# Top-32 attention with a routed expert layer on one core: VectorE's choices and weighting moved behind the rank, sums of marks made to wait for them

## The chip, the cores and the metric

One NeuronCore of a Trainium2 chip runs the whole kernel. The metric is the device time of one execution in microseconds. The kernel before was timed three times, 1264.31 to 1267.04 us, with a median of 1265.7 us.

## The reference

```python
scores = scale * np.matmul(q, k.transpose(0, 1, 3, 2))          # 8 batches, 8 heads, 576 x 576, depth 64
kth = np.partition(scores, -top_k, axis=-1)[..., -top_k:-top_k + 1]   # top_k = 32
scores = np.where(scores >= kth, scores, -1000000000.0)
attn = softmax(scores); x = attn @ v                             # rows of 512 = 8 heads x 64
logits = x @ w_gate; e_idx = np.argmax(logits, axis=1)           # one of 8 experts a row
out[rows of e] = gate_w * sigmoid(x @ w_output_gate)[e] * (relu(x @ w1[e]) @ w2[e])
```

Each of the 4608 rows keeps, for each head, its 32 largest scores of 576; the attention output is sent to the one expert that its gate prefers (512 to 1024 to 512, float32), weighted by the gate's probability and a sigmoid.

## The kernel before, in words

**Steps.** The rows form 36 tiles of 128 queries, the heads four pairs. A step `i` (the loop of line 919) is one tile and one pair of heads, 144 steps in all and four more for what trails behind. Every engine gets its instructions in the order in which the program writes them, so a step is an order written out by hand, in which pieces of neighbouring pairs are interleaved.

**A pair's way.** TensorE forms the scores of pair `i + 1` at the top of step `i` (`scores`, L293), ScalarE copies them out of PSUM (L301). VectorE takes the eight largest of each of eight groups of 72 columns (`gmax`, MAX8, L320), a step ahead. `rank(i)` draws from these the 24 largest scores in three rounds (MAX8 L328, MATCH_REPLACE8 L331). `below(i)`: ScalarE marks what lies below the 24th with a Sign and counts it (L355), GpSimd adds marks and scores to a sum (`w`, L358), and `window` takes eight more of the sum with a MAX8 over 576 columns (L370). `choose` picks the 32nd largest of the row by the count (two tiny SCALAR_TENSOR_TENSORs, L381); `weigh` multiplies the exponentials (`exps`, ScalarE, L365) by "score is at least the 32nd" and sums them (L397).

In the first 36 steps (`LONE`) the second head of a pair is weighted in another way: `choose` also writes the negated 32nd value (`less`, L385), `veil` has ScalarE make a Sign of score less that value (L404) and GpSimd add it to the score (L407), and `unveil` takes ScalarE's Exp of that with its sum (L413), one step later.

Two steps after its rank a pair is transposed by TensorE in three parts (`flip`, L423: four blocks, one, four), each copied out by ScalarE (L431); two PSUM buffers serve the three parts, so the third part waits for the copy of the first. `attend` (L455, every second step) multiplies by the values, and ScalarE copies the result (L457).

**The order inside a step before.** Scores of `i + 1`; rank of `i` with three fills (a fill runs one queued small operation of the routing); scaling of rows; `below(i)`; `unveil(i - 2)`; attend, flips, a piece of an expert (`heavy`), Exps of `i`; then on VectorE `window(i - 1)` twice, `gmax(i + 1)`, a fill, `choose(i - 1)`, a fill, `weigh(i - 1)`; then gathers and scatters; `veil(i - 1)`; three fills.

**Experts.** When a group of tiles has been attended, `route` queues the small operations of its routing. For each slot (128 rows of one expert) the two weight matrices are loaded by SP (`fetch_w1` L704, `fetch_w2` L709) as soon as the slot stands in `order`; the list of its rows (`fetch_id`, L721) and the rows themselves (`fetch_x`, a GpSimd gather, L729) follow, TensorE transposes them (`turn`, L739), and a slot is worked off in four pieces, one a step (`up` L750 twice, `down` L765 twice). `later` queues slow GpSimd work with an estimated cost and a due time, and `run_slow` runs it from a budget at each step. For the first two groups the slots are fixed; for the other six a slot table (`slot_table`, some 32 tiny GpSimd operations) says which expert a slot serves, and SP reads it for the loads. Before, `route` queues the scatters of row ids first and the table behind them, and `queue_slots` extends `order` when both are done. The last nine slots and some before them are worked off behind the 144 steps.

Of the kernel before, what the change touches and what calls it, by code (L numbers as in the profile page):

```python
# [16 lines left out]
ALU = mybir.AluOpType  # L17
# [6 lines left out]
P = 128  # L24
# [8 lines left out]
DMAS = 2.2  # L33
MORE = 3.2
# [5 lines left out]
def tile_topk_attention_moe(  # L40
# [11 lines left out]
    nc = tc.nc  # L52
# [25 lines left out]
    ids = dram.tile([NID, 4], I32, name="ids")  # L78
# [12 lines left out]
    ENDS, EARLY, LEAST = zip(*sorts) if sorts else ((), (), ())  # L91
# [103 lines left out]
    def run(exact, stack):  # L195
# [25 lines left out]
        def later(what, cost, f, due):  # L221
            queued[0] += 1
            slow.append((step[0] + due, queued[0], what, cost, f))
            slow.sort()

        def run_slow(budget, kinds):

            for x in [x for x in slow if x[2] in kinds]:
                if spent[0] + x[3] > budget:
                    return  # L230
                slow.remove(x)
                spent[0] += x[3]
                x[4]()
# [7 lines left out]
        def waiting(what):  # L241
            return any(x[2] == what for x in slow)

        def fill(n=1):
            for _ in range(n):
                if urgent:
                    urgent.popleft()()
                elif small and small[0]() is not False:
                    small.popleft()
# [96 lines left out]
        def below(i):  # L346
            vs = VV[i][0]
            ep = wk.tile([P, 2, S], F32, name="ep", bufs=3)
            EP[i] = ep
            if not exact:  # L350
                n = wk.tile([P, 2], F32, name="n", bufs=3)
                SW[i] = ([], n)
                for a in range(2):
                    s, m = SC[i, a], marks[a]
                    nc.scalar.activation(m.bitcast(I8).rearrange("p (s b) -> p s b", b=2)[:, :, 1], s, AF.Sign,  # L355
                                         bias=vs[:, a, PIVOT - 1:PIVOT], scale=-(1.0 + 2.0 ** -20), accum_out=n[:, a:a + 1])
                    w = wk.tile([P, S], F32, name="w", bufs=3)
                    nc.gpsimd.tensor_tensor(w, s, m, op=ALU.add)  # L358
                    SW[i][0].append(w)

        def exps(i):
# [5 lines left out]
        def window(i, a):  # L367
            if exact:
                return
            nc.vector.max(out=VV[i][0][:, a, 24:32], in_=SW[i][0][a])  # L370

        def kth_col(i, a):
            return VV[i][0][:, a, TOPK - 1:TOPK] if exact else KTH[:, 2 * i + a:2 * i + a + 1]

        def choose(i):
# [10 lines left out]

            nc.gpsimd.tensor_copy(NEAR[:, i], vs[:, :, PIVOT - 1:PIVOT + 2:2])

        def weigh(i):
            t, hp = divmod(i, NHP)  # L390
            if hp == 0:
                SM[t] = st.tile([P, H], F32, name="sums", bufs=3)
            for a in (0, 1):
                if lone(i, a):
                    return
                e = EP[i][:, a, :]
                nc.vector.scalar_tensor_tensor(e, SC.pop((i, a)), kth_col(i, a), e, op0=ALU.is_ge, op1=ALU.mult,  # L397
                                               accum_out=SM[t][:, 2 * hp + a:2 * hp + a + 1])
            del VV[i]

        def veil(i):
# [407 lines left out]
        def queue_slots(g, n, rows):  # L809
            flush("x")  # L810
            assert rows_done[0] >= rows
            if g not in FIXED:
                order.extend((g, k, rows) for k in range(n))
            listed[0] += n
            known[0] = step[0] + (0 if had["id"] == cur[0] and not heavy else 1)
# [3 lines left out]
        def ids_known():  # L819

            ahead("id", fetch_id, listed[0] - cur[0])
            assert had["id"] - cur[0] <= NLIST - 2
# [68 lines left out]
        scores(0)(((0, 1), (1, 2)))  # L891

        def route(g):
            small.extend(group_route(g, LGT[g]))
            if g < NGRP - 1:
                def some(part):
                    for f in part:
                        f()
                if g in FIXED:
                    order.extend((g, k, (GROUPS[g][-1] + 1) * P) for k in range(EARLY[g]))  # L900
                    parts = [settle(FIXED[g])]
                else:
                    ops = slot_table(g, False)
                    parts = [ops[x:x + 4] for x in range(0, len(ops), 4)]

                def tables():
                    for part in parts:
                        later("ids", 0.18 * len(part), lambda part=part: some(part), 1)
                small.append(tables)
                small.append(lambda: not waiting("ids"))  # L910
                small.append(lambda: queue_slots(g, EARLY[g], (GROUPS[g][-1] + 1) * P))
                small.append(lambda: step[0] >= known[0] and ids_known())

        LGT = {}
        gi = 0
# [3 lines left out]
        for i in range(NSTEP + 4):  # L919
            t, hp = divmod(i, NHP)  # L920
            step[0] = i
            if i + 1 < NSTEP:
                scores(i + 1)()
            for r in range(3):
                if i < NSTEP:
                    rank(i, r)
                    if r == 0:
                        shift(i)
                fill(1)
            spent[0] = 0.0  # L930
            run_slow(SUMS, ("x",))
            spent[0] = 0.0
            if i < NSTEP:
                below(i)
            if 2 <= i < NSTEP + 2:
                unveil(i - 2)
            early, late = [], []
            if 4 <= i < NSTEP + 4 and i % 2 == 0:
                early.append(attend(i - 4))
            if 2 <= i < NSTEP + 2:  # L940
                early.append(flip(i - 2, 0))
                early.append(flip(i - 2, 1, side_start()))
            if i >= NSTEP + 2:
                extra = side_start()
                if extra:
                    early.append(extra(ps_t.tile([P, 4, P], F32, name="pst")))

            room = not uses
            ahead_of_slot()
            heavy_start()  # L950
            ev = heavy_piece()
            if ev:
                late.append(ev)
            if 2 <= i < NSTEP + 2:
                late.append(flip(i - 2, 2))
            ev = turn_ahead() if room else None
            if ev:
                late.append(ev)
            for f in early:
                f()  # L960
            if i < NSTEP:
                exps(i)
            for f in late:
                f()
            if 1 <= i <= NSTEP:
                window(i - 1, 0)
                window(i - 1, 1)
            if i + 1 < NSTEP:
                gmax(i + 1, 0)
                gmax(i + 1, 1)  # L970
            fill(1)
            if 1 <= i <= NSTEP:
                choose(i - 1)
                fill(1)
                weigh(i - 1)
            ahead("x", fetch_x, 2, "id", 1)
            run_slow(DMAS if i < LONE else MORE, ("ids", "out"))
            if 1 <= i <= NSTEP:
                veil(i - 1)
            side_use()  # L980
            fill(3)
            if i < NSTEP:
                if hp == 0 and t + 2 < NTT:
                    load_q(t + 2)
                if i == 0:
                    small.extend(([] if exact else setup()) + [clear_ids])
                jj = t % 9
                b2 = t // 9 * 2
                for j0, b in ((0, b2 + 1), (5, b2 + 2)):
                    n = (jj - j0) * NHP + hp  # L990
                    if b < NB:
                        if n == 1:
                            load_k(b)
                        if n == 6:
                            load_v(b)
            if i >= 3 and (i - 3) % NHP == NHP - 1:
                tt = (i - 3) // NHP
                if tt == GROUPS[gi][0]:
                    LGT[gi] = st.tile([P, max(map(len, GROUPS)), 16], F32, name="lg", bufs=2)
                tile_rows(tt, gi, LGT[gi], tt - GROUPS[gi][0])  # L1000
                if tt == GROUPS[gi][-1]:
                    gi += 1
# [6 lines left out]
        def background():  # L1009
            step[0] += 1  # L1010
            extra = side_start()
            if extra:
                extra(ps_t.tile([P, 4, P], F32, name="pst"))()
                side_use()
            fill(60)
            run_slow(1e9, ("ids", "x", "out"))

        tail[0] = True
        HL = {}
# [149 lines left out]
```

## Time and profile before

| what | value |
|---|---|
| median of three executions | 1265.7 us |
| the profiled execution | 1265.68 us |
| its span, first to last instruction | 1263.8 us |
| mean granted TensorE clock | 0.956 |
| PE busy | 1158.3 us (92%) |
| DVE busy | 1121.2 us (89%) |
| ACT busy | 961.5 us (76%) |
| POOL busy | 704.9 us (56%) |

PE is TensorE's matmuls, PEld its weight loads, DVE is VectorE, ACT ScalarE, POOL GpSimd, SP the engine that issues most DMAs. A row of a timeline reads: start and length in us, engine, line of the kernel, operation, output<-inputs, shapes, count, and in brackets how long the engine had been idle before and what ended that. In the table by stage each engine's busy time stands with its number of instructions. An engine that waits inside an instruction's own span is counted as busy.

### The profile page before, as it was taken

What the parts mean: (1) busy time and instruction counts of PE and PEld (TensorE: products, weight loads), DVE (VectorE), ACT (ScalarE), POOL (GpSimd) and SP (SyncE); (2) the same over time, 40 slices, a digit from 0 to 9 for tenths busy, and PEclk for the clock granted to TensorE, in tenths of its full rate; (3) what the DMA queues carried; (4) which work ended last, traced back from release to release, by engine and by line L of the source; (5) the groups of instructions that cost most, each with busy time, mean ns of one, the idle gap of its engine ahead of it and who ended that gap; (6) DMA issues with size and microseconds to landing.
All of it is one profiled execution on the core that took longest, in us unless ns stands there. A gap on an engine that the chain in (4) does not pass through costs nothing.

```text
span 1263.8 us, 30889 instructions
## 1 busy us (share of the span) xinstructions
PE 1158.3 (92%) x9771; PEld 889.1 (70%) x9771; DVE 1121.2 (89%) x6097; ACT 961.5 (76%) x1896; POOL 704.9 (56%) x1120
## 2 busy tenths in 40 slices
PE   4776676779999999999999999999989999999996
PEld 3554454457777677777777777777767777799995
DVE  6999999999999999999999999999989996363442
ACT  5899998888888888888888888888868886354542
POOL 5666666774547765586654775554865583321110
PEclk7788778889999999999999999999989999999998
DMA  5400033535545665575656655764076446799980
GB/s 138 78 18 18 18 101 123 179 86 183 184 159 168 202 211 170 179 219 182 211 188 205 218 193 196 226 205 159 10 266 229 159 159 233 254 397 366 360 328 21
DMA packets 113734, 227.46 MB, mean 180 GB/s; under 512 B 19206, under 2 KB 37894, under 8 KB 112528
## 3 DMA queue, kind: packets, MB, share of 16 engines
q1 hardware_dynamic: 104176, 205.67, 48.6%
q0 software_dynamic: 7552, 18.96, 4.4%
q8 instruction: 81, 1.33, 0.4%
q10 hardware_dynamic: 1824, 0.67, 0.3%
q14 instruction: 101, 0.83, 0.2%
HBM read 206.68 MB, written 20.69 MB: 180 GB/s over the span
## 4 chain that ended last, share of the span: by engine, by line
PE 51%; DVE 31%; issue 11%; ACT 3%; DMA 2%; POOL 2%; POOLq 0%; SPq 0%; ACTq 0%
PE pm L750 13%; PE pm L765 11%; DVE cand L320 10%; PE ps L293 8%; PE pst L423 8%; PE po L455 8%; DVE v L370 5%; DVE ep L397 5%; DVE x L381 3%; DVE cand L331 3%; DVE v L328 3%; DMA w1t<-in_w_dram 1%; PE pst L476 1%; ACT marks L355 1%; ACT s L301 1%
## 5 line engine op out<-in xcount | busy, mean ns | idle before, releaser
L358 POOL TENSOR_TENSOR w<-s,marks 128x576 f32<-128x576 f32 x288 | 362.8, 1281 | 170.3 <-ACT marks L355 166.4
L320 DVE MAX8 cand<-s 128x8 f32<-128x72 f32 x2304 | 322.3, 218 | 18.4 <-ACT s L301 18.0
L750 PE MATMUL pm<-xs,w1t 128*128 128x128 f32 x2560 | 299.6, 276 | 4.5 <-DMA w1t<-in_w_dram 3.6
L750 PEld LDWEIGHTS pm<-xs,w1t 128*128 128x128 f32 x2560 | 294.3, 193 | 6.1 <-DMA w1t<-in_w_dram 3.8
L423 PE MATMUL pst<-ident,ep 128*128 128x128 f32 x1296 | 212.5, 289 | 83.1 <-ACT ep L413 70.4
L423 PEld LDWEIGHTS pst<-ident,ep 128*128 128x128 f32 x1296 | 149.5, 144 | 166.1 <-ACT ep L413 77.4
L355 ACT ACTIVATE marks<-s,v 128x576 int8<-128x576 f32 x288 | 220.4, 769 | 21.8 <-DVE v L328 16.6
L431 ACT ACTIVATE pT<-pst 128x512 f32<-128x512 f32 (+1 forms) x432 | 196.6, 484 | 23.3 <-PE pst L423 15.1
L301 ACT ACTIVATE s<-ps 128x1152 f32<-128x1152 f32 (+1 forms) x145 | 163.0, 1125 | 57.8 <-PE ps L293 57.5
L370 DVE MAX8 v<-w 128x8 f32<-128x576 f32 x288 | 202.1, 743 | 0.2 <-issue 0.2
L765 PE MATMUL pm<-w2t,ht 128*128 128x512 f32 x448 | 202.0, 594 | 0.0
L293 PE MATMUL ps<-kst,qst 64*128 64x288 f32 (+1 forms) x1280 | 193.4, 455 | 5.1 <-ACT s L301 5.1
L397 DVE SCALAR_TENSOR_TENSOR ep<-s,kth,ep 128x576 f32<-128x576 f32 x252 | 197.3, 814 | 0.3 <-issue 0.3
L455 PEld LDWEIGHTS po<-pT,v 128*64 128x64 f32 x3200 | 167.9, 144 | 32.6 <-issue 32.6
L365 ACT ACTIVATE ep<-s,v 128x576 f32<-128x576 f32 x252 | 184.1, 781 | 0.5 <-POOL v L344 0.5
L455 PE MATMUL po<-pT,v 128*64 128x128 f32 (+1 forms) x3200 | 184.4, 274 | 0.0
L776 POOL DMA_INDIRECT out_dram<-y,idt x40 | 49.0, 1224 | 176.8 <-ACT y L772 163.5
L293 PEld LDWEIGHTS ps<-kst,qst 64*128 64x128 f32 (+1 forms) x1280 | 103.2, 187 | 50.1 <-issue 25.7
L765 PEld LDWEIGHTS pm<-w2t,ht 128*128 128x128 f32 x448 | 80.9, 190 | 81.0 <-issue 81.0
L328 DVE MAX8 v<-cand 128x8 f32<-128x16 f32 (+2 forms) x864 | 129.2, 190 | 0.0
L381 DVE SCALAR_TENSOR_TENSOR x<-left,n,v 128x8 f32<-128x8 f32 x288 | 113.4, 429 | 0.0
L331 DVE MATCH_REPLACE8 cand<-v,cand 128x16 f32<-128x16 f32 (+1 forms) x576 | 95.1, 174 | 0.0
(167 smaller groups left out, 1200.1 us busy)
## 6 DMA issues: line engine op xcount, KB each, us to landing
w1t<-in_w_dram SPq DMA_DIRECT2D x40, 2048.0 KB, 9.2
w2t<-in_w_dram SPq DMA_DIRECT2D x40, 2048.0 KB, 11.0
x_rows<-xu SPq DMA_DIRECT2D x36, 256.0 KB, 2.2
qst<-in_qa_dram SPq DMA_DIRECT2D x70, 128.0 KB, 10.3
v<-in_va_dram SPq DMA_DIRECT2D x8, 1024.0 KB, 5.8
kst<-in_ka_dram SPq DMA_DIRECT2D x14, 576.0 KB, 5.7
v<-in_va_dram SPq DMA_DIRECT2D x16, 64.0 KB, 6.2
ids<-far SPq DMA_DIRECT2D x1, 678.0 KB
```

Of the source, the lines that this page charges most:

```text
L293: nc.tensor.matmul(ps[qs, a, n, :288], Q[t][rows, hp, qs], K[b][rows, hp, cols], start=True, stop=True)
L320: nc.vector.max(out=c[:, 8 * g:8 * g + 8], in_=SC[i, a][:, g * GW:(g + 1) * GW])
L355: nc.scalar.activation(m.bitcast(I8).rearrange("p (s b) -> p s b", b=2)[:, :, 1], s, AF.Sign, bias=vs[:, a, PIVOT - 1:PIVOT], scale=-(1.0 ...
L358: nc.gpsimd.tensor_tensor(w, s, m, op=ALU.add)
L365: nc.scalar.activation(EP[i][:, a, :], SC[i, a], AF.Exp, bias=VV[i][0][:, a, 32:33], scale=SCALE)
L370: nc.vector.max(out=VV[i][0][:, a, 24:32], in_=SW[i][0][a])
L397: nc.vector.scalar_tensor_tensor(e, SC.pop((i, a)), kth_col(i, a), e, op0=ALU.is_ge, op1=ALU.mult, accum_out=SM[t][:, 2 * hp + a:2 * hp + ...
L423: nc.tensor.transpose(ps[:, c - c0, :], pt[:, c * P:(c + 1) * P], ident)
L431: nc.scalar.activation(x, ps[:, :n, :], AF.Copy)
L455: nc.tensor.matmul(po[a * 64:(a + 1) * 64, k, qs], lhs, rhs, start=half and not k and not m, stop=(c == 3 and k == 1 and m == len(TT[t]) - 1))
L750: nc.tensor.matmul(ph[:, f - f0, :], w[:, c, f * P:(f + 1) * P], XS[s][:, c, :], start=(c == 0), stop=(c == NC - 1))
L765: nc.tensor.matmul(PY[s], HT[s][:, f, :], w[:, f, :], start=(f == 0), stop=(f == NF - 1))
```

## The change

In a step, `choose(i - 1)`, two fills and `weigh(i - 1)` now come right behind the rank of `i`, then `below(i)` and `veil(i - 1)`, and only then the scaling of rows and `unveil(i - 2)`. GpSimd's first sum of marks in a step gets a dependency on the weighting of the pair before. `window(i)` now ends step `i`, behind `gmax(i + 1)`. In `route`, for the groups that need a slot table, the table's operations (a kind of their own, `table`) are queued ahead of the scatters, and `order` is extended as soon as the table is done; for the two fixed groups the order of things stays.

```diff
@@ below
                     w = wk.tile([P, S], F32, name="w", bufs=3)
-                    nc.gpsimd.tensor_tensor(w, s, m, op=ALU.add)
+                    x = nc.gpsimd.tensor_tensor(w, s, m, op=ALU.add)
+                    if LAST[0]:
+                        tc.add_manual_dep(x.ins, LAST[0].ins.name,
+                                          mybir.DependencyInfo(mybir.DependencyClass.Sync, mybir.DependencyReason.DATA),
+                                          reason="the weighting goes first")
+                        LAST[0] = None
@@ weigh
-                nc.vector.scalar_tensor_tensor(e, SC.pop((i, a)), kth_col(i, a), e, op0=ALU.is_ge, op1=ALU.mult,
-                                               accum_out=SM[t][:, 2 * hp + a:2 * hp + a + 1])
+                LAST[0] = nc.vector.scalar_tensor_tensor(e, SC.pop((i, a)), kth_col(i, a), e, op0=ALU.is_ge, op1=ALU.mult,
+                                                         accum_out=SM[t][:, 2 * hp + a:2 * hp + a + 1])
@@ queue_slots
-            if g not in FIXED:
+            if g == NGRP - 1:
                 order.extend((g, k, rows) for k in range(n))
@@ route
-            small.extend(group_route(g, LGT[g]))
+            ops = group_route(g, LGT[g])
+            small.extend(ops[:-1])
...
                 def tables():
                     for part in parts:
-                        later("ids", 0.18 * len(part), lambda part=part: some(part), 1)
-                small.append(tables)
+                        later("table", 0.18 * len(part), lambda part=part: some(part), 1)
+
+                def chosen():
+                    order.extend((g, k, (GROUPS[g][-1] + 1) * P) for k in range(EARLY[g]))
+                if g in FIXED:
+                    chosen()
+                    small.extend([ops[-1], tables])
+                else:
+                    small.extend([tables, ops[-1], lambda: not waiting("table"), chosen])
                 small.append(lambda: not waiting("ids"))
+                small.append(lambda: not waiting("table"))
                 small.append(lambda: queue_slots(g, EARLY[g], (GROUPS[g][-1] + 1) * P))
@@ a step
                 fill(1)
+            if 1 <= i <= NSTEP:
+                choose(i - 1)
+                fill(2)
+                weigh(i - 1)
+            if i < NSTEP:
+                below(i)
+            if 1 <= i <= NSTEP:
+                veil(i - 1)
             spent[0] = 0.0
             run_slow(SUMS, ("x",))
             spent[0] = 0.0
-            if i < NSTEP:
-                below(i)
             if 2 <= i < NSTEP + 2:
                 unveil(i - 2)
...
-            if 1 <= i <= NSTEP:
-                window(i - 1, 0)
-                window(i - 1, 1)
             if i + 1 < NSTEP:
                 gmax(i + 1, 0)
                 gmax(i + 1, 1)
-            fill(1)
-            if 1 <= i <= NSTEP:
-                choose(i - 1)
-                fill(1)
-                weigh(i - 1)
+            if i < NSTEP:
+                window(i, 0)
+                window(i, 1)
             ahead("x", fetch_x, 2, "id", 1)
-            run_slow(DMAS if i < LONE else MORE, ("ids", "out"))
-            if 1 <= i <= NSTEP:
-                veil(i - 1)
+            run_slow(DMAS if i < LONE else MORE, ("table", "ids", "out"))
```

More of the change, by code (lines that the diff above doesn't have):

```diff
@@ L387, in choose @@
             nc.gpsimd.tensor_copy(NEAR[:, i], vs[:, :, PIVOT - 1:PIVOT + 2:2])
+        LAST = [None]
         def weigh(i):
@@ L899, in route @@
                 if g in FIXED:
-                    order.extend((g, k, (GROUPS[g][-1] + 1) * P) for k in range(EARLY[g]))
                     parts = [settle(FIXED[g])]
                 else:
-                    ops = slot_table(g, False)
-                    parts = [ops[x:x + 4] for x in range(0, len(ops), 4)]
+                    table = slot_table(g, False)
+                    parts = [table[x:x + 4] for x in range(0, len(table), 4)]
                 def tables():
                     for part in parts:
-                        later("ids", 0.18 * len(part), lambda part=part: some(part), 1)
-                small.append(tables)
+                        later("table", 0.18 * len(part), lambda part=part: some(part), 1)
[6 more added lines that the diff above has]
+                    small.extend([tables, ops[-1], lambda: not waiting("table"), chosen])
                 small.append(lambda: not waiting("ids"))
+                small.append(lambda: not waiting("table"))
                 small.append(lambda: queue_slots(g, EARLY[g], (GROUPS[g][-1] + 1) * P))
                 small.append(lambda: step[0] >= known[0] and ids_known())
+            else:
+                small.extend(ops[-1:])
         LGT = {}
@@ L1015, in background @@
             fill(60)
-            run_slow(1e9, ("ids", "x", "out"))
+            run_slow(1e9, ("table", "ids", "x", "out"))
         tail[0] = True
```

## The prediction

> **What bounds the kernel now.** I read the page first for the span and the slices, then a table by stage, then the list of waits, and then the timelines of two places.
>
> ```profile
> span 1263.8 us, 30889 instructions
> PE   4776676779999999999999999999989999999996
> DVE  6999999999999999999999999999989996363442
> PEclk7788778889999999999999999999989999999998
> ```
>
> The slices show three stages: up to slice 8 VectorE is full and TensorE is not, and its clock is below full; then both are full; in the last six slices VectorE is half idle. The table by stage has the figures.
>
> ```profile
> 57.00:260.00 203.00, 142.15 (x1277) 99.11 (x1275) 198.56 (x1178) 183.12 (x389) 134.51 (x174) 0.84 0.22 71
> 305.00:1053.00 748.00, 742.43 (x6540) 559.63 (x6539) 740.24 (x4253) 612.12 (x1249) 466.78 (x782) 1.00 0.57 190
> 1053.00:1264.00 211.00, 197.79 (x1414) 175.09 (x1412) 92.26 (x146) 87.90 (x106) 43.71 (x59) 0.98 0.77 282
> ```
>
> Columns: length, then busy time of PE, weight loads, DVE, ACT and POOL, then the granted clock. I call the first stretch the veiled stage: there the second head of a pair is weighted by ScalarE (veil, unveil) and no expert work runs yet. The second is the mixed stage, the third the tail.
>
> In the mixed stage PE idles 748 - 742.43 = 5.6 us in all. Is a busy PE there a PE at its pace? One product block in the mixed stage, beside one of the tail:
>
> ```profile
> 947.09 3.74 PE L750 MATMUL pm<-xs,w1t 128*128 128x128 f32 x32
> 1109.80 6.19 PE L750 MATMUL pm<-xs,w1t 128*128 128x128 f32 x54
> ```
>
> 3.74/32 is 117 ns a matmul, 6.19/54 is 115 ns in the tail, where DVE is busy 92.26 of 211 us and cannot hold PE back. So the mixed stage goes at PE's pace, and a faster DVE is worth there at most the 5.6 us. The veiled stage has no such bound: PE is busy 142.15 of 203 us. Whom does it wait for?
>
> ```profile
> PE pst L423 <- ACT ep L413: 70.4, 26, 4.9
> PE pm L750 <- DMA w1t<-in_w_dram: 3.6, 1, 3.6
> ```
>
> Nearly all of its idle time ends with unveil (L413), ScalarE's Exp of the veiled head. ACT itself is busy 183.12 of the 203 us, so the stage can't become shorter than by 20 us.
>
> **The change part by part. 1. The stall that it removes.** The choices (L381) are tiny, yet some take long:
>
> ```profile
> L381 DVE SCALAR_TENSOR_TENSOR x<-left,n,v x288: 186/218/1972, 18.7 to 1061.7; 128x8 f32<-128x8 f32 x144
> 57.00:260.00 203.00, 25.32 (x116) 0.84 0.22 71
> 305.00:1053.00 748.00, 74.09 (x404) 1.00 0.57 190
> 711.89 2.25 DVE L320 MAX8 cand<-s 128x8 f32<-128x72 f32 x16 [0.19 <-ACT s L301]
> 712.68 2.52 POOL L358 TENSOR_TENSOR w<-s,marks 128x576 f32<-128x576 f32 x2 [1.37 <-ACT marks L355]
> 714.06 1.17 DVE L381 SCALAR_TENSOR_TENSOR x<-left,n,v 128x8 f32<-128x8 f32 x1
> ```
>
> The first row gives minimum, median and maximum in ns; the next two are L381's busy time by stage (four records a step, so 29 and 101 steps, 7.00 and 7.41 us each). In the timeline the choice starts at 714.06 and holds DVE until 715.23, while POOL's two sums end at 715.20: it waits, inside its own span, for POOL to end. MAX8s run beside the same sums undelayed (16 in 2.25 us). Two free choices take some 2 x 0.186 = 0.37 us, so the stalls are 25.32 - 29 x 0.37 = 14.6 us in the veiled stage and 74.09 - 101 x 0.37 = 36.7 us in the mixed one. Choices and weighting now stand behind the rank, and the sums wait for the weighting, so nearly all 51 us vanish from DVE. In the mixed stage that is worth nothing: PE covers it, and DVE will be seen idle before its MAX8s over scores (L320, waiting for ACT) instead. If that cover were gone it would be worth up to 36.7 us (a rival below).
>
> **2. The new wait.** POOL's first sum of a pair waits for the last weighting. Behind it on POOL stand the second sum, the veil's sum, the scaling of rows, the scatters and gathers, and the next shift, for which ACT's Exp waits. And the MAX8s over the sums now end the same step. Does that chain fit into a step?
>
> ```profile
> 701.73 0.24 DVE L328 MAX8 v<-cand 128x8 f32<-128x16 f32 x2
> 703.07 1.40 DVE L370 MAX8 v<-w 128x8 f32<-128x576 f32 x2
> L397 DVE SCALAR_TENSOR_TENSOR ep<-s,kth,ep 128x576 f32<-128x576 f32 x252 | 197.3, 814 | 0.3 <-issue 0.3
> ```
>
> Rank 703.07 - 701.73 = 1.34, choices 0.37, two weightings 1.63 at most, POOL's sums 2.52, the second MAX8 0.70: 6.56 us, and DVE's own work 1.34 + 0.37 + 1.63 + 2.25 + 1.40 = 6.99 against a step of 7.41. It fits with 0.4 us to spare; where POOL is late by more (slot tables, gathers that wait for their list) DVE is late by the rest. POOL is busy 466.78 of 748 us, so that is seldom: 0 to +5 us over seven groups, and I take +1.
>
> **3. The veil's sign is moved ahead of unveil on ACT.** This is the part that I expect to cost. One whole cycle of the veiled stage, ACT's rows and the two PE blocks it hangs on:
>
> ```profile
> 161.13 1.13 ACT L301 ACTIVATE s<-ps 128x1152 f32<-128x1152 f32 x1 [0.20 <-PE ps L293]
> 162.16 0.77 ACT L355 ACTIVATE marks<-s,v 128x576 int8<-128x576 f32 x1
> 163.68 0.76 ACT L413 ACTIVATE ep<-w,v 128x576 f32<-128x576 f32 x1
> 164.44 0.37 ACT L457 ACTIVATE xT<-po 128x256 f32<-128x256 f32 x1
> 164.91 0.77 ACT L431 ACTIVATE pT<-pst 128x512 f32<-128x512 f32 x2
> 165.56 0.66 PE L423 MATMUL pst<-ident,ep 128*128 128x128 f32 x4 [0.58 <-ACT pT L431]
> 165.56 0.78 ACT L365 ACTIVATE ep<-s,v 128x576 f32<-128x576 f32 x1
> 166.14 1.24 PE L293 MATMUL ps<-kst,qst 64*128 64x288 f32 x8
> 166.25 0.60 ACT L431 ACTIVATE pT<-pst 128x512 f32<-128x512 f32 x1
> 166.74 0.77 ACT L404 ACTIVATE marks<-s,less 128x576 int8<-128x576 f32 x1
> 167.43 1.13 ACT L301 ACTIVATE s<-ps 128x1152 f32<-128x1152 f32 x1
> ```
>
> PE's last transposes (165.56) need ACT's copy of the first ones, which ACT has queued behind unveil; the next scores (166.14) stand behind them on PE; ACT's copy of these scores, at 167.43, comes 0.05 us after they end. Meanwhile ACT does the Exp, a copy and the veil's sign (166.74 to 167.43): today the sign lies in the shadow of PE's transposes and scores and costs nothing. In the changed order it stands behind the two signs of L355 and ahead of unveil. Then the loop is: copy of scores 1.03 (161.13 to 162.16), two signs 1.52 (to 163.68), veil's sign 0.69, unveil 0.76, copies until PE may go on 1.12 (164.44 to 165.56), transposes 0.58, scores with hand-over 1.29: 6.99 us, where this cycle took 6.30. In steps without L457 (every second) 0.47 less, 6.52; mean 6.75. This is with PE at full clock; the clock is not:
>
> ```profile
> 144.62 1.06 PE L423 MATMUL pst<-ident,ep 128*128 128x128 f32 x4
> 145.62 2.29 PE L293 MATMUL ps<-kst,qst 64*128 64x288 f32 x8
> 170.88 0.33 PE L423 MATMUL pst<-ident,ep 128*128 128x128 f32 x1 [2.91 <-ACT ep L413]
> ```
>
> At 145 us the same blocks take 2.29 and 1.06 us instead of 1.24 and 0.66: 1.45 us more on the loop, at half rate. A mean clock of 0.84 is half rate for (1 - 0.84)/0.5 = 32% of the time, so 0.46 us a step on average. 6.75 + 0.46 = 7.21 against 7.00 now: +0.21 a step, and 36 steps are veiled: +7.6, with a slower start of the first steps (the MAX8s over the first sums come before the second rank) +8. DVE's 14.6 us of stall turn into waiting for ACT. The bounds: if this loop doesn't bind, at best the 20 us above; if the half rate becomes twice as frequent, 0.46 x 36 = 17 us more.
>
> **4. Tables ahead of scatters.** For six groups the slot table is computed, and the order of slots extended, before the ids are scattered. So the weights of a group's first slots are asked for on SP's queue some steps earlier, ahead of the id lists; SP may stand there until POOL has made the table, with the next query loads, wanted only eight steps later, behind it. What that is worth:
>
> ```profile
> 921.70 4.43 SPq L721 DMA_DIRECT2D idt<-ids  x5
> 926.65 0.38 SPq L704 DMA_DIRECT2D w1t<-in_w_dram  x1
> 936.01 6.13 PE L750 MATMUL pm<-xs,w1t 128*128 128x128 f32 x32 [3.60 <-DMA w1t<-in_w_dram]
> ```
>
> The weights are issued at 926.65, behind five id lists, and PE waits 3.60 us for them; the block then takes 6.13 instead of 3.74 us, since the clock had dropped (slice 30). Together 6.0 us, at this one place (the list of waits has no other of the kind). An issue only 6 us earlier suffices: -6. If the order slips a step elsewhere, 3 us either way (a product block of 3.74 us that is missed in a step). The other 2 us of PE's idle time in the mixed stage may go too: -1. The budgets under a new name and the changed number of fills move no more than these.
>
> Sum: +1 + 8 - 6 - 1 = +2 us. The profiled execution took 1265.68 us (1.9 beside its span), the median is 1265.7. Forecast: 1268 us.
>
> **The rivals.** *A, faster: DVE's stall does pace the veiled stage.* For it: DVE is busy 198.56 of 203 us there. Against it: ACT has 183.12 us of work and the loop above has its own length. Its price: half of the 20 us at most, and the 6 us of the weights, 1250 (1243 to 1259).
>
> *B, much faster: the mixed stage is DVE's.* DVE is busy 740.24 of 748 us there, PEld 559.63. The Trainium skill (Perfetto Trace Analysis, Identifying the Most-Contended Engine) says that busy matmul time says little of how near TensorE is to its limit, and that weight loads should be read instead; by that PE has a quarter free. The 117 against 115 ns above speak against it here. If it holds, 36.7 us of stall and the 6 us return: about 1225.
>
> *C, slower: the clock.* PE idles 2.91 us before the row at 170.88, and full rate was lost in the first nine slices, at slice 30 and in the last one, each time with PE idle for a while. The moved sign makes this gap 2.91 + 0.69 = 3.6 us. If that turns half rate from 32 to 55% of the stage, 0.23 x 1.45 x 36 = 12 us more: 1280 (1277 to 1286). It decides from about 45%. The Trainium skill (TensorE: Matmul & The Clock Gate, HAM oscillation) says that idle gaps beyond about 3 us between bursts throttle the clock to half; by that rule this rival would be likelier than I give it, as the 2.91 us are just below.
>
> *D, slower: part 4 doesn't do what it says.* The order is extended earlier, but SP's queue or a buffer of weights is not free in time: the 6 us stay, 1274 (1271 to 1277).
>
> **How the numbers follow.** About 0.2% (2.5 us) is what a measurement of this kernel tells from no change. My case has a chance of 0.55, from 1262 to 1274: 0.04 of it faster, 0.27 within, 0.24 slower. A has 0.21, B 0.04, C 0.12, D 0.08. So faster 0.04 + 0.21 + 0.04 = 0.29, the same 0.27, slower 0.24 + 0.12 + 0.08 = 0.44. The range 1254 to 1279 leaves out B, half of A and half of C.
>
> **What would show it.** Right: L381's maximum near its median; in the veiled stage steps of 7.1 to 7.4 us, DVE with gaps before L320 that ACT ends, PE's wait for L413 longer than 70.4 us; in the mixed stage PE as full as now, and no wait of L750 for w1t near 930 us. Wrong: veiled steps below 6.9 us (A), a mixed stage below 735 us for 101 steps (B), a clock below 0.78 in the veiled stage (C), the wait for w1t still there (D), or DVE waiting for POOL's sums (L358) in many mixed steps.

## The result and the profile after

| | before | after |
|---|---|---|
| median of five executions each, on the same chip | 1266.35 us (1264.31 to 1270.35) | 1280.31 us (1276.63 to 1283.05) |
| the profiled execution | 1265.68 us | 1280.13 us |
| mean granted clock | 0.956 | 0.957 |

The ratio is 1.0108 (95% interval 1.0081 to 1.0135): the change makes the kernel 1.1% slower, where 1268 us was forecast. First the span and slices of the kernel after.

```profile
span 1278.3 us, 30831 instructions
PE   5667766669999999999999999999999999999996
DVE  6888888889999999999999999999999995364542
PEclk7888888889999999999999999999999999999998
```

The dip of the clock at slice 30 is gone, VectorE is no longer full in the veiled stage, and PE isn't fuller there. The table by stage has the same columns as before (PE, weight loads, DVE, ACT, POOL, then the clock):

```profile
57.00:260.00 203.00, 136.57 (x1193) 93.35 (x1192) 175.78 (x1098) 170.78 (x364) 122.92 (x157) 0.85 0.22 70
305.00:1053.00 748.00, 745.60 (x6584) 561.62 (x6583) 712.52 (x4272) 616.48 (x1260) 480.05 (x784) 1.00 0.57 189
```

In 203 us of the veiled stage every engine now does less (PE 1193 matmuls for 1277): the stage goes slower, while no engine is full and the mean clock is as it was. In the mixed stage DVE has 28 us less to do and PE is as full as before. The border between the stages is the first product block of an expert, here in the timeline of before and then of after:

```profile
278.64 3.74 PE L750 MATMUL pm<-xs,w1t 128*128 128x128 f32 x32
```

```profile
297.33 3.74 PE L757 MATMUL pm<-xs,w1t 128*128 128x128 f32 x32
```

It comes 18.7 us later. From there to the end of the span it is 1278.3 - 297.33 = 981.0 us for 985.2, so 4.2 us come back, and 14.5 us of the span remain lost. The list of waits of the whole execution of after says who waits for whom (total, times, longest):

```profile
PE pst L430 <- ACT ep L420: 87.0, 36, 7.9
POOL w L358 <- DVE ep L404: 72.0, 30, 3.0
DVE cand L320 <- ACT s L301: 37.4, 35, 7.6
```

L430 and L420 are the flip and unveil (L423 and L413 before): 87.0 us for 70.4. In the 203 us of the veiled stage alone the three waits are 58.9 us (55.6 before), 10.5 and 15.8 (3.1 before, at L320). One cycle of two steps in the timeline of after:

```profile
181.29 0.76 ACT L411 ACTIVATE marks<-s,less 128x576 int8<-128x576 f32 x1
181.96 0.76 ACT L420 ACTIVATE ep<-w,v 128x576 f32<-128x576 f32 x1
182.87 0.48 PE L430 MATMUL pst<-ident,ep 128*128 128x128 f32 x1 [3.58 <-ACT ep L420]
...
184.34 1.06 PE L430 MATMUL pst<-ident,ep 128*128 128x128 f32 x4
185.33 2.29 PE L293 MATMUL ps<-kst,qst 64*128 64x288 f32 x8
187.55 2.96 PE L462 MATMUL po<-pT,v 128*64 128x128 f32 x40
187.67 1.13 ACT L301 ACTIVATE s<-ps 128x1152 f32<-128x1152 f32 x1 [1.22 <-PE ps L293]
188.83 2.25 DVE L320 MAX8 cand<-s 128x8 f32<-128x72 f32 x16 [2.01 <-ACT s L301]
...
191.79 0.33 PE L430 MATMUL pst<-ident,ep 128*128 128x128 f32 x1 [0.69 <-ACT ep L420]
...
193.12 1.24 PE L293 MATMUL ps<-kst,qst 64*128 64x288 f32 x8
194.41 1.13 ACT L301 ACTIVATE s<-ps 128x1152 f32<-128x1152 f32 x1 [0.23 <-PE ps L293]
...
198.53 0.33 PE L430 MATMUL pst<-ident,ep 128*128 128x128 f32 x1 [3.58 <-ACT ep L420]
...
200.06 2.29 PE L293 MATMUL ps<-kst,qst 64*128 64x288 f32 x8
```

The veil's sign (L411) stands ahead of unveil (L420), as the change has it. In the odd step PE is idle for 3.58 us, and then its four transposes take 1.06 and its scores 2.29 us: half rate. ACT waits 1.22 us for these scores and VectorE 2.01 us for ACT. In the even step attend (L462) fills part of PE's wait, the gap is short, and the same scores take 1.24 us. At 198.53 it starts over, with the same 3.58 us. Before, the gaps of odd steps were mostly 2.9 or 3.3 us by turns, with the 2.91 that the prediction took at the lower end. Of the 29 score blocks of pairs 8 to 36, 9 take over 2 us before (31%); after, 13 do (45%), which is every second one but one where a batch ends. The steps take 7.54 us on average (from 65.81 to 269.41 us in 27 steps) where the prediction had 7.21.

The other signs that the prediction named: the choices (now L386) no longer stall, the list by line gives a largest one of 577 ns for 1972; and PE doesn't wait for weights at the place that was near 930 us. First the choices, then SP's queue, then PE:

```profile
L386 DVE SCALAR_TENSOR_TENSOR x<-left,n,v x288: 204/220/577, 16.7 to 1073.1; 128x8 f32<-128x8 f32 x144
```

```profile
913.96 0.04 SPq L711 DMA_DIRECT2D w1t<-in_w_dram  x1
930.57 5.58 SPq L728 DMA_DIRECT2D idt<-ids  x5
```

```profile
951.66 3.74 PE L757 MATMUL pm<-xs,w1t 128*128 128x128 f32 x32
```

The weights are issued 16.6 us ahead of the id lists, and the same product block (the 45th) runs without a wait in 3.74 us, where it waited 3.60 us and took 6.13. One sign against the forecast is there too: in the mixed stage VectorE's MAX8s over the sums (L375) wait for POOL's sums (L358) 47 times, 24.0 us in all; TensorE stays full beside it.

### The profile page after: what moved, and what is told of

Its sections match the earlier page's. It is cut to its first block, busy times and chain, and to the rows that moved or that the text cites. A ratio compares the mean times of both kernels' runs of the same rounds, so it can differ in the third digit from the quotient of the medians.

```text
span 1278.3 us, 30831 instructions
## 1 busy us (share of the span) xinstructions
PE 1161.5 (91%) x9771; PEld 887.2 (69%) x9771; DVE 1071.7 (84%) x6097; ACT 960.5 (75%) x1896; POOL 715.7 (56%) x1120
## 4 chain that ended last, share of the span: by engine, by line
PE 66%; issue 12%; ACT 8%; DVE 6%; POOL 5%; DMA 1%; POOLq 0%; ACTq 0%; DVEq 0%
PE pm L757 15%; PE pm L772 14%; PE ps L293 12%; PE pst L430 11%; PE po L462 10%; ACT marks L355 4%; POOL w L358 3%; PE pst L483 2%; ACT ep L420 1%; DVE cand L331 1%; ACT marks L411 1%; DVE v L328 1%; PE pst L492 1%; PE pst L746 1%; DVE v L375 1%
## 5 line engine op out<-in xcount | busy, mean ns | idle before, releaser
L358 POOL TENSOR_TENSOR w<-s,marks 128x576 f32<-128x576 f32 x288 | 362.7, 1280 | 286.8 <-ACT marks L355 205.8
L320 DVE MAX8 cand<-s 128x8 f32<-128x72 f32 x2304 | 324.1, 219 | 38.1 <-ACT s L301 37.4
L430 PE MATMUL pst<-ident,ep 128*128 128x128 f32 x1296 | 215.9, 291 | 96.4 <-ACT ep L420 87.0
L430 PEld LDWEIGHTS pst<-ident,ep 128*128 128x128 f32 x1296 | 151.0, 145 | 180.1 <-ACT ep L420 95.8
L375 DVE MAX8 v<-w 128x8 f32<-128x576 f32 x288 | 210.6, 749 | 41.4 <-POOL w L358 38.0
L438 ACT ACTIVATE pT<-pst 128x512 f32<-128x512 f32 (+1 forms) x432 | 196.7, 484 | 25.0 <-PE pst L430 14.5
L293 PE MATMUL ps<-kst,qst 64*128 64x288 f32 (+1 forms) x1280 | 197.9, 464 | 5.1 <-ACT s L301 5.1
L404 DVE SCALAR_TENSOR_TENSOR ep<-s,kth,ep 128x576 f32<-128x576 f32 x252 | 197.8, 817 | 0.9 <-ACT ep L370 0.8
L462 PEld LDWEIGHTS po<-pT,v 128*64 128x64 f32 x3200 | 164.5, 141 | 33.8 <-issue 33.4
L462 PE MATMUL po<-pT,v 128*64 128x128 f32 (+1 forms) x3200 | 181.2, 270 | 0.0
L293 PEld LDWEIGHTS ps<-kst,qst 64*128 64x128 f32 (+1 forms) x1280 | 105.9, 192 | 52.2 <-issue 27.5
L1055 DVE TENSOR_TENSOR w2l<-w2t,w2h 128x2048 fp32r<-128x2048 f32 x24 | 54.4, 2291 | 25.0 <-ACT w2h L1054 25.0
```

The costliest lines, as they stand in the source:

```text
L293: nc.tensor.matmul(ps[qs, a, n, :288], Q[t][rows, hp, qs], K[b][rows, hp, cols], start=True, stop=True)
L320: nc.vector.max(out=c[:, 8 * g:8 * g + 8], in_=SC[i, a][:, g * GW:(g + 1) * GW])
L358: x = nc.gpsimd.tensor_tensor(w, s, m, op=ALU.add)
L404: LAST[0] = nc.vector.scalar_tensor_tensor(e, SC.pop((i, a)), kth_col(i, a), e, op0=ALU.is_ge, op1=ALU.mult, accum_out=SM[t][:, 2 * hp + a ...
L430: nc.tensor.transpose(ps[:, c - c0, :], pt[:, c * P:(c + 1) * P], ident)
L438: nc.scalar.activation(x, ps[:, :n, :], AF.Copy)
```

## The experiments

Each kernel was timed in five rounds beside the kernel before on the same chip, to which the ratios are. This table puts them side by side; "first block" is the start of the first product block in the kernel's profile, "rest" the span less that.

| kernel | ratio | clock | first block, us | rest, us |
|---|---|---|---|---|
| before | 1 | 0.956 | 278.6 | 985.2 |
| after | 1.0108 | 0.957 | 297.3 | 981.0 |
| after, the veil moved back | 0.9966 | 0.958 | 279.5 | 979.9 |
| VectorE's order and the wait alone | 0.9991 | 0.957 | 281.2 | 983.6 |
| before, the tables' order alone | 1.0040 | 0.957 | 277.1 | 993.0 |
| after, without the wait | 1.0488 | 0.949 | 297.0 | 1029.3 |
| after, 8 fillers in odd steps | 1.0033 | 0.965 | 290.0 | 981.8 |
| after, 16 fillers | 0.9958 | 0.982 | 279.1 | 981.9 |
| after, 22 fillers | 0.9937 | 0.981 | 277.6 | 980.9 |
| after, 22 fillers in even steps | 1.0211 | 0.961 | 311.8 | 982.2 |
| after, the veil moved back, 16 fillers | 0.9916 | 0.980 | 272.8 | 980.3 |
| before, 16 fillers | 0.9901 | 0.980 | 266.9 | 986.1 |
| both orders, 16 fillers | 0.9862 | 0.984 | 268.4 | 980.5 |

A filler is a transpose of the identity matrix into a PSUM block that the flip's own transpose overwrites at once; nobody reads it.

**1. The veil moved back.**

```diff
@@ a step (of after)
                 below(i)
-            if 1 <= i <= NSTEP:
-                veil(i - 1)
...
             run_slow(DMAS if i < LONE else MORE, ("table", "ids", "out"))
+            if 1 <= i <= NSTEP:
+                veil(i - 1)
```

> The changed kernel with one move undone: the veil (ScalarE's Sign of the veiled head and GpSimd's sum of it) goes back behind the gathers and scatters, so that unveil again comes right behind the two signs on ScalarE; choices, weighting, windows, the dependency and the tables stay as changed. Theory 1 (the veil's sign ahead of unveil stretches TensorE's idle gap before the second flip from 2.9 to 3.6 us, and the half rate that follows falls on the flips and scores that the step waits for): the time up to the first expert matmul falls from 297 us to 275 to 280 us, the whole to 1258 to 1264 us, faster than both kernels. Rival 2 (the sums waiting for the weighting, and the MAX8s over sums in the same step, hold VectorE back): the veiled stage keeps its 7.5 us a step, about 1280 us.

Measured: 1264.4 us, ratio 0.9966 (0.9954 to 0.9978), at the upper end of what was expected. The first block comes at 279.5 us, the rest takes 979.9. So the moved veil is the whole loss, and without it the change is a little faster than before. What remains to be told apart is the veil's length on ACT and the clock.

**2. The tables alone.** The diff of `route`, `queue_slots` and the budgets in the kernel before, VectorE's order left as it was.

> The kernel before with the tables alone: slot tables queued ahead of the scatters and the order of slots extended when the table is done; VectorE's and ScalarE's order stays as before. Theory: the wait of TensorE for the first weights near 930 us (3.60 us, and 2.4 us of half rate behind it) goes, nothing else changes: 1260 us against 1266. Rival: the scatters that now come behind the table delay the id lists, a step somewhere goes without a piece of an expert, and the gain is lost: 1264 to 1268 us.

Measured: 1273.3 us, ratio 1.0040 (1.0027 to 1.0054): slower, and outside both of the expected ranges. The rest takes 993.0 us for 985.2. SP's queue and PE in that kernel:

```profile
899.37 0.38 SPq L704 DMA_DIRECT2D w1t<-in_w_dram  x1
922.38 4.42 SPq L721 DMA_DIRECT2D idt<-ids  x5
```

```profile
950.83 1.12 PE L423 MATMUL pst<-ident,ep 128*128 128x128 f32 x4 [3.05 <-ACT pT L431]
```

The weights are early, as wanted (899.37), but the id lists come at 922.38, no earlier than before (921.70), and their rows can't be gathered before them; GpSimd's gather behind them comes at 931.42 for 924.27. The three steps that begin at 932.7, 937.7 and 944.5 us have no expert piece, PE idles there and behind (3.05 us in the row shown), and their pieces go into the tail, which takes 226.3 us behind the last scores for 217.9. The gain of the tables isn't there without VectorE's new order.

**3. Work in the gap.** Is it the longer chain on ACT, or the clock that the gap takes down?

```diff
@@ flip (of after), ahead of the transposes of part 1
+            if part == 1 and lone(i, 1) and i % 2:
+                for _ in range(22):
+                    nc.tensor.transpose(ps[:, 0, :], ident, ident)
```

> The changed kernel with 22 more transposes of the identity in every second veiled step, on TensorE ahead of the second flip, into the PSUM tile that this flip then overwrites: about 2.4 us of matmuls that nobody reads, in the gap of 3.58 us. Theory 1 (it is the half rate, falling on the same blocks every second step): the granted clock of the veiled stage goes from 0.85 to over 0.95, the scores there take 1.24 instead of 2.29 us, the time to the first expert matmul falls by 15 to 25 us, the whole to 1255 to 1265 us. Rival 3 (the longer order of ScalarE alone, at whatever clock): nothing changes or it becomes slower, 1278 to 1284 us.

Measured: 1260.9 us, ratio 0.9937 (0.9925 to 0.995). The table by stage and the odd step:

```profile
57.00:260.00 203.00, 160.87 (x1611) 123.46 (x1613) 189.84 (x1185) 182.47 (x390) 135.00 (x175) 0.97 0.23 73
```

```profile
184.29 2.57 PE L431 MATMUL pst<-ident 128*128 128x128 f32 x22
188.03 0.33 PE L433 MATMUL pst<-ident,ep 128*128 128x128 f32 x1 [1.18 <-ACT ep L420]
...
189.10 1.24 PE L293 MATMUL ps<-kst,qst 64*128 64x288 f32 x8
```

PE waits for the same unveil, with 1.18 us of idle time for 3.58, and the scores behind it take 1.24 us for 2.29. The veiled stage is 19.7 us shorter with the veil still in its new place. So the chain's length alone can't be the loss.

**4. Without the wait.** The five lines in `below` taken out.

> The changed kernel without the added dependency of the sums on the weighting (it orders only; no data hang on it). Theory 1: the veiled stage is bound by ScalarE and TensorE and stays at 7.5 us a step, with the sums the weightings now wait inside their span (medians of 0.8 us, some 2 us and more), the mixed stage stays at TensorE's pace: 1276 to 1284 us. Rival 2 (the wait is what costs): faster by over 5 us, under 1275 us.

Measured: 1328.6 us, ratio 1.0488 (1.0466 to 1.0511): against the kernel after, 1.0488 - 1.0108 = 0.038, 48 us more. It lies behind the first block (1029.3 us for 981.0). In its timeline POOL's sums and the second weighting run at the same time:

```profile
699.80 3.06 POOL L358 TENSOR_TENSOR w<-s,marks 128x576 f32<-128x576 f32 x2 [1.66 <-ACT marks L355]
...
699.89 1.83 DVE L399 SCALAR_TENSOR_TENSOR ep<-s,kth,ep 128x576 f32<-128x576 f32 x1
```

The two sums take 3.06 us for the 2.52 alone, the weighting 1.83 us for 0.81. Over the whole execution the weightings take 260.3 us for 197.8 and the sums 392.6 for 362.7. The busy times from 320 to 1050 us, without the wait and then of after:

```profile
320.00:1050.00 730.00, 693.46 (x6050) 516.93 (x6049) 706.45 (x3923) 561.23 (x1151) 456.56 (x703) 0.99 0.55 182
```

```profile
320.00:1050.00 730.00, 727.60 (x6442) 547.93 (x6441) 695.52 (x4177) 603.19 (x1233) 471.83 (x774) 1.00 0.58 193
```

PE has 34 us more of idle time without the wait, of which 32.8 end with small operations of VectorE for the routing (L513, L553); VectorE spends more time on fewer instructions, and in the chain that ended last it has 34% of the span for 6%. My expectation was wrong here: the wait isn't a small cost, without it the new order loses 48 us. The stall of the choices comes back as a larger one of the weightings.

**5. How much filler, and where.** The edit of 3 with 8 and with 16 transposes, and with 22 in even steps.

> The changed kernel with 8 unread transposes instead of 22 in the gap of odd veiled steps. Theory (full rate is lost when PE is idle for more than about half of a window of 3.4 us): 8 of them, about 0.9 us, leave a gap of 2.6 us and split it, so some odd steps keep full rate and some don't: clock 0.87 to 0.95, 1266 to 1277. If any work in the gap is enough: clock above 0.95 and 1260 to 1263 as with 22. If the sum of work has to be high: clock 0.85, 1279 to 1283.

> The changed kernel with 16 unread transposes in odd veiled steps, between the 8 and 22 tried. Theory (half rate sets in when PE is busy for less than about 0.45 of a window of 3.4 us): 16 are 1.9 us, enough in most steps: clock 0.93 to 0.97, 1261 to 1266; the difference to the same with the veil moved back (1256.4) is then what the veil's place costs at full clock, 2 to 5 us. Rival (as with 8, a part of the steps): clock near 0.9, 1266 to 1271.

> The changed kernel with the 22 unread transposes in even veiled steps instead of odd ones, so that the same work is added where the gap of 3.58 us isn't. Theory (it is the gap before the first transposes of odd steps that sets half rate on the blocks behind it): clock of the veiled stage stays near 0.85 to 0.9, steps 7.4 to 7.6, 1276 to 1285. Rival (any added work of TensorE lifts the clock, wherever it stands): clock above 0.95 and 1259 to 1263 as with the odd steps.

Measured: 8 give 1272.4 us, ratio 1.0033 (1.0022 to 1.0044); 16 give 1262.6, 0.9958 (0.9943 to 0.9972); 22 in even steps 1295.1, 1.0211 (1.0192 to 1.0229). The odd step with 8, with 16, and of the kernel with the fillers in even steps:

```profile
167.16 0.33 PE L433 MATMUL pst<-ident,ep 128*128 128x128 f32 x1 [2.70 <-ACT ep L420]
...
168.50 2.29 PE L293 MATMUL ps<-kst,qst 64*128 64x288 f32 x8
```

```profile
187.46 0.33 PE L433 MATMUL pst<-ident,ep 128*128 128x128 f32 x1 [1.83 <-ACT ep L420]
...
188.52 1.24 PE L293 MATMUL ps<-kst,qst 64*128 64x288 f32 x8
```

```profile
190.39 0.48 PE L433 MATMUL pst<-ident,ep 128*128 128x128 f32 x1 [3.58 <-ACT ep L420]
...
192.85 2.29 PE L293 MATMUL ps<-kst,qst 64*128 64x288 f32 x8
```

With 8 fillers the gap of 2.70 us is still followed by half rate, at least in part, in 11 of 12 cases; with 16 the gap of 1.83 us is in 3 of 12. In the wrong steps the fillers leave the gap and its half rate, and stand in the way of real transposes on top; that this costs 13 us more than after (1.0211 - 1.0108) was not in my expectation. It is TensorE's work in the odd steps' wait, not the sum of its work, that counts.

The gap's length alone is not the rule, though: in the kernel before, gaps of 2.91 to 2.93 us were followed by half rate in two of six cases, less often than the 2.70 us here. The traces show a rule that fits all of this. In their records of the granted clock it changes only on a grid of 3.41 us. Here are four stretches of that grid, of after and then of before; a row has the length, PE's busy time, the number of its instructions and the clock (then two figures of the DMAs):

```profile
175.09:178.50 3.41, 1.95 (x13) 1.00 1.04 207
178.50:181.91 3.41, 0.79 (x6) 1.00 0.64 115
181.91:185.33 3.42, 2.46 (x15) 0.50 0.00 0
185.33:188.74 3.41, 3.41 (x21) 0.50 0.00 0
```

```profile
162.62:166.03 3.41, 2.83 (x65) 1.00 1.07 203
166.03:169.45 3.42, 1.94 (x14) 1.00 0.03 6
169.45:172.86 3.41, 1.98 (x19) 1.00 0.00 0
172.86:176.27 3.41, 3.41 (x50) 1.00 0.00 0
```

After, the gap of 3.58 us that ends at 182.87 leaves 0.79 us of work in one stretch, and the next two run at half rate. Before, the gap of 2.91 us that ends at 170.88 is split between two stretches; PE is busy for more than half of each (1.94 and 1.98 us), and the clock stays. From 57 us to the scores of pair 37, in all 13 traces, 92 stretches at full rate had PE busy for less than 0.45 of their length, and each was followed by half rate; 418 had more than 0.57, and none was; the 79 between went either way. Full rate came back 121 times, each time behind a stretch with PE busy for at least 0.93 of it.

**6. The same fillers without the veil's move, and without any change.**

> The changed kernel with the veil's sign back behind the gathers and scatters, and in odd veiled steps 16 transposes of the identity that nobody reads, put where PE waits for unveil. Theory (the half rate sits on the loop's blocks, with the old order too, since PE still idles some 2.9 us there): the granted clock of the veiled stage goes from about 0.85 to above 0.95 and the steps from 7.07 to 6.7 to 6.9 us, 24 steps or more of 0.2 to 0.35: 5 to 10 us below the 1264.4 of the veil moved back, 1254 to 1259. Rival 1 (with the old order VectorE or ScalarE paces the veiled steps, the clock is a symptom): clock up, steps unchanged, 1262 to 1266. Rival 2 (the extra transposes stand in the way of PE's real work): slower than 1266.

> The kernel before with nothing of the change, and the same 16 unread transposes in odd veiled steps. Theory (half rate costs the kernel before about 0.46 us a step on average, as the prediction took it): up to 36 x 0.46 = 16 us, of which VectorE's 14.6 us of stalls and its 198.6 us of busy time in 203 leave little room: 2 to 8 us less, 1258 to 1265. Rival (VectorE's stalls pace the veiled stage before, so that a faster PE frees nothing): 1266 to 1269 with a clock above 0.95.

Measured: with the veil moved back 1256.4 us, ratio 0.9916 (0.9897 to 0.9934), as expected; the kernel before with fillers 1255.6 us, 0.9901 (0.9885 to 0.9917), more than expected. Half rate had cost the kernel before 12.6 us already (0.0099 of 1268), though VectorE is nearly full there: its 203 us of the veiled stage with fillers are

```profile
57.00:260.00 203.00, 157.86 (x1573) 118.62 (x1573) 201.60 (x1215) 188.64 (x401) 140.21 (x182) 0.96 0.24 75
```

with 201.60 us of VectorE; it had time for 1215 instructions instead of 1178. With VectorE's new order and the veil in its old place the first block comes 6.0 us later than with the old order (272.8 for 266.9), and the stall is as large as with the old order. The timeline of that kernel:

```profile
196.48 1.28 POOL L414 TENSOR_TENSOR w<-s,marks 128x576 f32<-128x576 f32 x1 [1.91 <-ACT marks L411]
196.63 1.14 DVE L386 SCALAR_TENSOR_TENSOR x<-left,n,v 128x8 f32<-128x8 f32 x1
```

The veil's own sum (L414) on POOL now meets the choice, which takes 1.14 us for 0.22. The choices of this kernel take 23.39 us of the stage, those of the kernel before with fillers 22.74; after has 11.63 and before 25.32. With the veil ahead, that stall goes, at the price of the gap. The stall is thus not what makes the new order 6.0 us longer here.

**7. VectorE's order alone.** The veil and the tables as before.

> Of the change VectorE's new order and the added wait alone: the veil where it was, tables behind scatters as before. Theory (mixed stage is PE's, so VectorE's 36.7 us of stalls are worth nothing there, and the wait for the weights near 930 us stays): veiled steps about 7.05, the first expert block near 279.5, from there to the end about 985 as in the kernel before: 1266 to 1270, no different from before within 0.2%. Rival (the new order and not the tables brought the 4 to 5 us behind the first expert block): 979 to 981 from the first block on, 1263 to 1265, as with the tables changed.

Measured: 1267.9 us, ratio 0.9991 (0.9982 to 1.0): no difference, as expected in sum. One reason was wrong: the wait for the weights near 930 us is gone here too, since the lists come earlier (913.69 and not 921.70):

```profile
913.69 4.41 SPq L728 DMA_DIRECT2D idt<-ids  x5
918.66 0.38 SPq L711 DMA_DIRECT2D w1t<-in_w_dram  x1
```

The rest is 983.6 us: by one profile of each kernel, 1.6 of the 4.2 us come from VectorE's order, the others only with both.

**8. Both orders.** VectorE's order of before in the 36 veiled steps, the new one from step 36 on, the tables as changed, the veil in its old place, 16 fillers.

```diff
@@ a step
-            if 1 <= i <= NSTEP:
+            if LONE <= i <= NSTEP:
                 choose(i - 1)
...
+            if 1 <= i < LONE:
+                window(i - 1, 0)
+                window(i - 1, 1)
             if i + 1 < NSTEP:
                 gmax(i + 1, 0)
                 gmax(i + 1, 1)
+            if i < LONE:
+                fill(1)
+                if 1 <= i:
+                    choose(i - 1)
+                    fill(1)
+                    weigh(i - 1)
-            if i < NSTEP:
+            if LONE - 1 <= i < NSTEP:
                 window(i, 0)
```

> VectorE's order of before in the 36 veiled steps and the changed order from then on, with the veil where it was, the tables changed and the 16 unread transposes in odd veiled steps. Theory (with full clock the old order is the faster one in the veiled stage, first expert block at 266.8 with 6.84 us a step; the changed order and tables are the faster from there on, 980.3 against 986.1): 267 + 980.5 + 1.9 = about 1250, 1248 to 1253. Rival (the gain behind the first expert block hangs on how the veiled stage left the queues, or the 6 us at the start were chance): 1254 to 1258, as the two kernels with 16 transposes that it is put together from.

Measured: 1250.6 us, ratio 0.9862 (0.9844 to 0.988), 17.5 us less than before and the fastest kernel of the study. The first block at 268.4 and the rest of 980.5 us are close to those of the two kernels that it is made of (266.9 and 980.3).

## Why the prediction was wrong, point by point

Slower was the likelier side of the forecast and the veil's move its largest cost, but the size was missed, and the result lies just above the range. By the ratios (times 1268 us), the loss of 13.7 us adds up on the way from before to after by the kernels with the veil moved back and with 16 fillers: all but the veil 0.9966 - 1, -4.3; the veil's place at nearly full clock 0.9958 - 0.9916, +5.3; half rate 0.0150 after (1.0108 - 0.9958) for 0.0050 with the veil moved back (0.9966 - 0.9916), +12.7. By the intervals of the ratios each term is known to some 2 us; with 22 fillers instead of 16 in the changed kernel (0.9937) the last two would be +2.7 and +15.3.

*The step that failed* is the one of part 3 that took "half rate for (1 - 0.84)/0.5 = 32% of the time, so 0.46 us a step on average" and left it as it was in the changed kernel. The price of a block at half rate was right (2.29 for 1.24 us), and so was the share for the kernel before, where 9 of 29 score blocks (31%) were hit. To carry that share over was wrong: after the move 13 of 29 are hit, while the stage's mean clock is 0.85 for 0.84. The gap stands just ahead of the loop's blocks, and with 3.58 us practically every odd step is hit. Half rate costs 19.0 us there, 0.53 a step over 36 steps, and 12.7 us of it came with the move, where I had nothing. The count bears that out: with the veil moved back 7 of 29 are hit, so the move brings six more, by the prediction's 1.45 us a hit 6/29 x 36 x 1.45 = 10.8 us. This is rival C in its gap (3.6 us), its price (12 us, 1280) and in the 45% of half rate from which it was to decide, read as a share of the loop's blocks. As a share of the stage, as it was written, half rate stayed at (1 - 0.85)/0.5 = 30%; so its price was right in part by luck, and its test, "a clock below 0.78", would have ruled it out. The row at 170.88 that it pointed to was itself not followed by half rate: the scores behind it, at 172.30, took 1.24 us.

The chain's own length in part 3 was not far off: +8 expected, 5.3 measured at nearly full clock (2.7 by the kernel with 22 fillers). Its sentence that DVE's stall in the veiled stage turns into waiting for ACT is right (15.8 us before L320 in the 203 us, for 3.1).

What the forecast lacked besides, without harm here: VectorE's order itself makes the veiled stage longer. At nearly full clock the first block comes 6.0 us later with it (272.8 for 266.9); at the clock as it is only 0.9 (279.5 for 278.6), where also fewer score blocks are hit by half rate (7 for 9). Half rate costs the kernel before 12.6 us, and the kernel with VectorE's order, the tables and the veil moved back 6.3. The kernel with both orders gets 4.4 of the 6.0 back. What in the new order costs them is not isolated; the stall is not it (23.39 and 22.74 us of choices).

*Part 1* was right: the stalls went (the choices take 54.1 us in all for 113.4), and in the mixed stage this is worth nearly nothing, 28 us less of VectorE and PE as full as before. That speaks against rival B; the Trainium skill's rule (Perfetto Trace Analysis, Identifying the Most-Contended Engine), by which TensorE had a quarter free, isn't borne out by this trace. But the cover is thin: in the kernel without the wait VectorE's larger stalls do slow the stage.

*Part 2* isn't isolated, but its size fits: POOL waits 72.0 us for weightings and DVE then 24.0 us for POOL in the mixed stage, the sign named as speaking against it, and yet from the first block on nothing is lost. What I hadn't seen is its use, the 48 us of experiment 4.

*Part 4*: the 6.0 us at 930 us went as foreseen (from the 44th to the 46th product block 30.2 us, 930.12 to 960.34, for 35.9, 911.24 to 947.09). The sum of parts 1, 2 and 4 behind the first block was -6; 4.2 us are measured. But the tables alone don't bring it (experiment 2: +7.8 us); they need the earlier id lists of VectorE's order, issued 633.2 us behind the first block after (930.57 - 297.33) and 632.5 with that order alone, for 643.1 before and 645.3 with the tables alone.

*Rival A* had VectorE's stall as the pace of the veiled stage. Fillers alone, with the choices still at 22.74 us there, take 12.6 us off, so at the clock of before the stall was not the whole pace. A clean test is missing: VectorE's order alone gains nothing, but it leaves 20.37 us of choices in the stage, and the kernels without the stall all have the veil ahead. With fillers VectorE is as good as full (201.60 of 203 us), so there the stall may well count. *Rival D* didn't happen.

The Trainium skill (TensorE: Matmul & The Clock Gate, HAM oscillation) has idle gaps beyond about 3.4 us throttle the clock. The trace agrees for 3.58 us; but gaps of 2.70 us do the same here, so a short gap is no safety: what fits is TensorE's busy share in the stretches of 3.41 us of experiment 5. By that page's rule rival C deserved more than its 0.12.

## What to carry to other kernels

A stage's mean clock doesn't say which blocks run at half rate: compare the durations of the same block on the critical loop, step by step, and look at TensorE's work in the few microseconds ahead of it. An instruction moved ahead of the one that TensorE waits for costs some of its own length (here 5.3 us for 36 signs of 0.69) and, if TensorE is left idle long enough, the doubled time of what follows (12.7 us); a few transposes that nobody reads can be cheaper than the gap. And an order of instructions that is good in one stage can be worse in another: here each stage wanted its own.

## What the runs showed of the hardware that was not expected

VectorE's SCALAR_TENSOR_TENSOR takes longer when it overlaps GpSimd's sum over 128x576: the tiny choice 1.14 us for 0.22, the weighting 1.83 for 0.81. Beside the weighting two sums take longer too, 3.06 us for 2.52; beside the choice the sum keeps its 1.28. Sixteen MAX8s beside the same sums keep their 2.25 us. Which of these is put beside POOL's sums decides 48 us here.

A clock at half rate needs more work to come back than it needed to stay: 0.45 to 0.57 of a stretch of 3.41 us decided whether full rate was kept, and none of the 45 stretches at half rate with PE busy for less than 0.93 of them was followed by full rate.
